# Issuing the selection's transfers from ScalarE instead of SyncE, with a new order of issue

## The chip, the cores and the metric

One core of one Trainium2 chip runs the kernel. The metric is the device time of one execution in microseconds. The kernel before was timed three times: 409.54, 410.28 and 411.35 us, median 410.28 us. One further execution was taken with the hardware profiler.

The engines are called PE (TensorE, the matmuls; PEld are its weight loads), DVE (VectorE), ACT (ScalarE), POOL (GpSimd) and SP (SyncE, which only issues transfers here). Each engine takes its instructions from a queue of its own, strictly in order; "SPq" marks what SP's queue does.

## The reference

Eight sequences of 3136 tokens with 256 channels are filtered in the frequency domain. In each filtered sequence the 128 tokens with the highest scores then go through a small two-layer network.

```python
X = np.fft.rfft(x, axis=1)                       # x: 8 x 3136 x 256
y = np.fft.irfft(X * (filt_r + 1j * filt_i)[None], n=3136, axis=1)
scores = np.einsum('bsd,d->bs', y, w_gate)
out = y.copy()
for b in range(8):
    top = np.argpartition(-scores[b], 128)[:128]  # capacity 128
    xe = y[b, top]
    ye = np.maximum(xe @ w1, 0.0) @ w2            # 256 -> 1024 -> 256
    out[b, top] = xe + sigmoid(scores[b, top])[:, None] * ye
```

## The kernel before, in words

**The filter.** A sequence is cut as 98 x 32 tokens, so that the transform is a product of small matrices. For one batch (one sequence) the work runs as follows. `load` (L506) brings two halves of X, 2 MB together. In eight chunks of 32 channels `outer` (L384) folds X (`add`, `sub`, L401, mostly on POOL), multiplies it (`amm`, L413 to L424, PE) and transposes it into UU (`tout`, L427, DVE). `inner` (L292) takes UU in seven groups: a product (`zmm`, L314, PE), its evacuation to q (`zout`, L318, ACT), two products with the filter (`pmul`, L328, DVE, and `qmul`, L331, POOL), the back transform (`vmm`, L347, PE), its evacuation (`vout`, L361, ACT) and the scores (`gate`, L372, DVE). Then `outer` transposes again (`tin`, L398, DVE), multiplies (`f1`, `f2`, L435, PE, with a two-column copy `fence`, L440, on ACT between them) and evacuates into X (`yout`, L443, ACT), and `store` (L502) writes the half of X out. X exists once: a half is loaded only after its last content was stored. Batch 7 takes a variant of the last step (`fe`, L450, with evacuations `odd`, L458 and L464, on ACT). Three batches are in work at a time: one is loaded and folded, one is filtered, one is transformed back.

**The selection.** `select` (L532) finds the 128 best of a sequence, for batches 0 to 2 together, 3 to 5 together, 6 alone and 7 alone. After the scores are transposed and turned into integer keys in two parts (`s0` to `s5`, DVE and ACT, key tile `kf`), three steps move data:
- `s6` (L583) writes the keys to the buffer `scr` in device memory, in two transfers.
- `s7` (L589) reads `scr` back into the tile `R`, one transfer for each batch of the group and part of the key. Each copies the rows of keys to many partitions. A group of three batches reads its high parts here; batches 6 and 7 read both parts.
- `s8` (L684), for the two groups of three only, reads the low parts into the same `R`, when the high parts are done.

These are 24 transfers: 8 of `s6`, 10 of `s7`, 6 of `s8` (both of the latter in `spread_rows`, L599 to L602). `s7` has to wait until `s6`'s transfers have landed, and until `R` is free. Between them lies a search in rounds: `count` (L627, ACT) counts over `R`, `total` (PE) sums, `over` (L650, L651) and `nextd` set the next threshold. In the middle of the rounds `f8` (L661) and `upper` (L665), both on ACT, finish the high parts, `s8` replaces them in `R`, and `lower` (L669, DVE) adds what `upper` left. The rounds run beside the filter of later batches. Steps `c0` to `c11` then turn the thresholds into row numbers (`idx`).

**The network.** `weights` loads w1 and w2 at the end of the filter, ACT splits them (`whi`, L860) and POOL takes the remainders (`wlo`). `ffn` gathers the selected rows (POOL, indirect transfers, L887), turns them (`turn`, `turned`, L901), multiplies (`up`, L921, and `down`, L946), with `relu` (L931) on ACT, and scatters the result (L954). Batches 0 to 2 begin at about 335 us, while batch 7 is still transformed back.

**The order.** Every step is an entry of the list `prog`, in the order in which `op` is called. `ORDER` (L138) is a hand-fixed list of all 1536 entries: the order in which they are issued, and so the order on each engine's queue. `RINGS` (L212) says for each product which of four PSUM buffers it takes. The entries that matter here: 527, 528, 552 are `s6`, `s7`, `s8` of batches 0 to 2; 989, 990, 1014 those of batches 3 to 5; 1167, 1168 are `s6`, `s7` of batch 6; 1272, 1273 those of batch 7. Of ACT: 1075 and 1068 are the first two `zout` of batch 7, 1012 and 1013 are `f8` and `upper` of batches 3 to 5, 978 and 1120 are `yout` of batches 5 and 6, 620 is a `zout` of batch 4, 1342 is one of the eight `whi`, 1360 the first `relu`. Of SP: 393 loads the second half of batch 4, 517 stores that of batch 2.

Of the kernel before, what the change touches and what calls it, by code (L numbers as in the profile page):

```python
# [47 lines left out]
def _tables(C):  # L48
# [172 lines left out]
def kernel(  # L221
# [310 lines left out]
    def select(bs, st, sts):  # L532
# [50 lines left out]
        def s6():  # L583
            st["scr"] = scr = drm.tile([2, 4, S], F32, name="scr", bufs=2)
            for t in range(2):
                nc.sync.dma_start(out=scr[t, :G].rearrange("g (a c) -> a g c", c=N2),
                                  in_=st[KF][:, t, :GW].rearrange("a (g c) -> a g c", c=N2))
# [523 lines left out]
```

## Time and profile before

| What | us |
|---|---|
| three timed runs | 409.54, 410.28, 411.35 (median 410.28) |
| the profiled execution, its own time | 409.91 |
| its span, first to last instruction | 408.1 |
| PE busy | 384.0 (94%) |
| DVE busy | 348.0 (85%) |
| POOL busy | 306.0 (75%) |
| ACT busy | 239.6 (59%) |
| mean granted clock of TensorE | 0.999 |

The span leaves 409.91 - 408.1 = 1.81 us outside of it. Busy time counts neither waiting nor the issuing of transfers. A matmul's end is modelled, and so 94% does not mean that PE could do no more. Idle time is given in brackets, before the instruction that ended it, with the engine and the line of what it waited for.

### The profile page before, as it was taken

Reading aid. Unit: us, or ns where it says so; the run is one execution under the profiler, and the core shown is the slowest. Engines: PE = TensorE matmul, PEld = TensorE weight load, DVE = VectorE, ACT = ScalarE, POOL = GpSimd, SP = SyncE. Lnnn points to the kernel's source line nnn. Section 1 sums busy time; section 2 is a strip of 40 time slices with the busy share of each in tenths; the row PEclk is TensorE's granted clock in tenths of the full one; section 3 lists DMA queues with packets and bytes.
Section 4 is the critical chain, followed back from the end, with each engine's and each line's share of the span. In section 5 each row is a group of like instructions: output and inputs, shape, how many; then the busy total and the mean of one; then the engine's idle time right before and its main releaser. Section 6 shows DMA issues by size and latency. Waiting matters only on the chain.

```text
span 408.1 us, 11556 instructions
## 1 busy us (share of the span) xinstructions
PE 384.0 (94%) x4666; PEld 215.3 (53%) x4666; DVE 348.0 (85%) x902; ACT 239.6 (59%) x442; POOL 306.0 (75%) x218
## 2 busy tenths in 40 slices
PE   8979799999999999899999999999998989989894
PEld 6445434555544544353454453575344435859794
DVE  2868999989999998879799999999987799888632
ACT  1155235655556578867675554567889985486211
POOL 2367999999897999399959895999179664773262
PEclk9999999999999999999999999999999999999999
DMA  7999950725663654674824565824063556107811
GB/s 287 416 385 411 410 189 32 304 112 208 233 244 145 230 224 180 244 262 188 308 92 207 208 236 230 324 76 207 5 250 118 156 209 246 41 28 214 225 45 34
DMA packets 21957, 83.30 MB, mean 204 GB/s; under 512 B 3472, under 2 KB 13456, under 8 KB 18576
## 3 DMA queue, kind: packets, MB, share of 16 engines
q1 hardware_dynamic: 20912, 80.47, 52.1%
q0 software_dynamic: 992, 2.10, 1.7%
q8 instruction: 37, 0.61, 0.6%
q14 instruction: 16, 0.13, 0.1%
HBM read 47.76 MB, written 34.80 MB: 202 GB/s over the span
## 4 chain that ended last, share of the span: by engine, by line
PE 56%; POOL 10%; DVE 10%; DMA 8%; ACT 7%; issue 7%; SPq 1%; POOLq 0%; ACTq 0%; DVEq 0%
PE ps L435 16%; PE ps L347 13%; PE ps L423 8%; PE ps L314 6%; PE ps L946 4%; PE ps L921 4%; DMA tf_sb<-in_tf_dram 3%; POOL q L331 3%; DMA X<-in_x_dram 2%; POOL X L401 2%; POOL s L401 2%; ACT X L443 2%; DVE rj L372 2%; DMA fb_sb<-in_fri_dram 2%; DVE UU L427 2%
## 5 line engine op out<-in xcount | busy, mean ns | idle before, releaser
L331 POOL TENSOR_TENSOR q<-q,fb_sb 128x1024 f32<-128x1024 f32 (+1 forms) x56 | 119.7, 2142 | 35.4 <-ACT q L318 34.8
L435 PE MATMUL ps<-t,c_sb 64*49 64x512 f32 (+1 forms) x896 | 113.0, 594 | 2.4 <-ACT t L440 1.2
L401 POOL TENSOR_TENSOR s<-X 113x512 f32<-113x512 f32 x57 | 72.5, 1278 | 19.2 <-DMA X<-in_x_dram 15.0
L427 DVE STREAM_TRANSPOSE UU<-ps 128x1024 f32<-128x1024 f32 x64 | 78.3, 1232 | 7.4 <-PE ps L423 7.0
L398 DVE STREAM_TRANSPOSE t<-UU 128x1024 f32<-128x1024 f32 x64 | 78.0, 1226 | 4.7 <-PE ps L435 3.0
L372 DVE SCALAR_TENSOR_TENSOR rj<-ps,wg_sb 128x256 bf16<-128x256 f32 x192 | 69.5, 419 | 9.6 <-PE ps L347 6.6
L443 ACT COPY X<-ps 113x1024 f32<-113x1024 f32 x56 | 56.1, 1012 | 35.0 <-PE ps L435 16.7
L423 PE MATMUL ps<-X,c_sb 49*64 49x512 f32 x324 | 72.4, 595 | 0.5 <-DMA c_sb<-in_cst_dram 0.5
L401 POOL TENSOR_TENSOR X<-X 113x512 f32<-113x512 f32 x53 | 67.5, 1279 | 3.3 <-DVE s L401 0.6
L361 ACT COPY UU<-ps 128x1024 f32<-128x1024 f32 x48 | 48.5, 1012 | 34.4 <-PE ps L347 26.9
L328 DVE TENSOR_TENSOR y<-ps,fa_sb 128x1024 f32<-128x1024 f32 (+1 forms) x56 | 61.2, 1099 | 6.3 <-DMA fa_sb<-in_fri_dram 3.0
L423 PE MATMUL ps<-s,c_sb 49*64 49x512 f32 x244 | 63.1, 596 | 3.5 <-DVE UU L427 2.2
L318 ACT COPY q<-ps 128x1024 f32<-128x1024 f32 (+1 forms) x56 | 51.6, 922 | 21.5 <-PE ps L314 13.0
L347 PE MATMUL ps<-y,ti_sb 64*64 64x256 f32 x768 | 61.2, 380 | 2.8 <-DVE y L328 1.5
L347 PE MATMUL ps<-q,ti_sb 64*64 64x256 f32 x768 | 60.4, 376 | 0.0
L314 PE MATMUL ps<-UU,tf_sb 64*64 64x256 f32 x768 | 52.2, 389 | 2.9 <-DVE UU L427 1.4
L435 PEld LDWEIGHTS ps<-t,c_sb 64*49 64x49 f32 (+1 forms) x896 | 30.5, 125 | 43.2 <-ACT t L440 12.9
L347 PEld LDWEIGHTS ps<-y,ti_sb 64*64 64x64 f32 x768 | 29.3, 132 | 26.1 <-issue 3.9
L314 PEld LDWEIGHTS ps<-UU,tf_sb 64*64 64x64 f32 x768 | 28.4, 132 | 25.0 <-issue 4.6
L347 PEld LDWEIGHTS ps<-q,ti_sb 64*64 64x64 f32 x768 | 30.9, 133 | 11.8 <-POOL q L331 0.9
L423 PEld LDWEIGHTS ps<-s,c_sb 49*64 49x64 f32 x244 | 15.9, 132 | 26.2 <-issue 11.9
L887 POOL DMA_INDIRECT fb_sb<-out_dram,idx x15 | 14.5, 968 | 18.7 <-DVE jk L794 15.3
(132 smaller groups left out, 456.8 us busy)
## 6 DMA issues: line engine op xcount, KB each, us to landing
out_dram<-X SPq DMA_DIRECT2D x16, 2048.0 KB
X<-in_x_dram SPq DMA_DIRECT2D x12, 2048.0 KB
X<-in_x_dram SPq DMA_DIRECT2D x16, 512.0 KB
fb_sb<-in_fri_dram SPq DMA_DIRECT2D x5, 512.0 KB
fa_sb<-in_fri_dram SPq DMA_DIRECT2D x5, 512.0 KB
fb_sb<-in_moe_w_dram SPq DMA_DIRECT2D x2, 1024.0 KB
R<-scr SPq DMA_DIRECT2D x12, 98.0 KB
ti_sb<-in_ti_dram SPq DMA_DIRECT2D x1, 832.0 KB
```

Of the source, the lines that this page charges most:

```text
L314: nc.tensor.matmul(z[o, hi, k * D:k * D + D], lhsT=tf_sb[p, l], rhs=urow(b, l, 0, D)[p], start=True, stop=True)
L318: nc.scalar.copy(out=q[:, :, :n * HW], in_=h["z"][:, :, :n * HW])
L328: nc.vector.tensor_tensor(out=part(y), in0=part(h["z"]), in1=filt(fa_sb), op=ALU.mult)
L331: nc.gpsimd.tensor_tensor(out=part(h["q"]), in0=part(h["q"]), in1=filt(fb_sb), op=ALU.mult)
L347: nc.tensor.matmul(v[o, j, k * D:k * D + D], lhsT=ti_at[p, t, i, hi], rhs=h["yq"[t]][p, hi, k * D:k * D + D], start=t == 0, stop=t == 1)
L372: nc.vector.scalar_tensor_tensor(out=rj, in0=h["v"][:, j, k * D:k * D + D], scalar=1.0, in1=wg_sb, op0=ALU.mult, op1=ALU.mult, accum_out=u ...
L398: nc.vector.transpose(out=h["t"].rearrange("p d (l j) -> p d l j", j=2), in_=uchan(b_out, c))
L401: (nc.gpsimd if fold[k] == "p" else nc.vector).tensor_tensor(out=out, in0=two[0], in1=two[1], op=(ALU.add, ALU.subtract)[k])
L423: nc.tensor.matmul(a[q, w].rearrange("p (n d) -> p n d", d=CW), lhsT=lhs[p], rhs=rhs[p], start=n == 0, stop=n == len(terms) - 1)
L427: nc.vector.transpose(out=uchan(b_in, c), in_=h["a"].rearrange("p w (n d) -> p d n w", d=CW))
L435: nc.tensor.matmul(h["f"][q, s], lhsT=cc["wi"][p, n], rhs=h["t"][p, s * 16:s * 16 + 16].rearrange("p d n -> p (d n)"), start=t == 0, stop= ...
L443: nc.scalar.copy(out=X[:RW2, hx, :, at], in_=h["f"][:RW2].rearrange("p s (d n) -> p n s d", n=N2))
```

## The change

The transfers of `s6`, `s7` and `s8` are issued by `nc.scalar`, that is by ACT's queue, in place of `nc.sync`, SP's queue. What they move is the same. The three steps count as ACT's, so that they stand in ACT's order. `ORDER` and `RINGS` are new: the same 1536 entries, of which most of the others stay where they were or move by a few places on their engine's queue. The diff, with those lines of the old and the new `ORDER` that hold the moved entries (and entry 1075), and without the rest of the list and `RINGS`:

```diff
...
-    451, 522, 398, 397, 406, 452, 523, 524, 484, 409, 453, 407, 525, 399, 410, 526, 408, 527, 412, 416, 400, 411, 467,
...
-    613, 513, 551, 607, 615, 514, 552, 515, 614, 606, 516, 675, 608, 616, 517, 619, 618, 663, 609, 620, 553, 664, 617,
...
-    877, 925, 983, 917, 984, 881, 985, 868, 986, 923, 927, 987, 885, 869, 952, 988, 919, 882, 989, 886, 934, 870, 938,
...
-    1074, 1010, 1164, 1165, 1011, 975, 1166, 1012, 1076, 1167, 1013, 968, 976, 1014, 1075, 977, 1116, 969, 1077, 1067,
...
-    1124, 1035, 1109, 1326, 1125, 1131, 1092, 1110, 1149, 1036, 1111, 1112, 1037, 1132, 1328, 1094, 1327, 1334, 1168,
...
-    1339, 1270, 1360, 1365, 1157, 1052, 1271, 1366, 1053, 1272, 1361, 1226, 1219, 1367, 1054, 1227, 1368, 1055, 1220,
...
-    1175, 1060, 1381, 1176, 1237, 1382, 1177, 1061, 1362, 1273, 1363, 1178, 1063, 1062, 1420, 1238, 1179, 1369, 1370,
...
+    451, 522, 398, 397, 406, 452, 523, 524, 484, 409, 463, 407, 525, 399, 410, 526, 408, 527, 412, 416, 400, 411, 467,
+    417, 401, 464, 453, 468, 393, 528, 469, 418, 419, 413, 470, 466, 430, 415, 454, 420, 431, 471, 456, 414, 455, 432,
...
+    605, 550, 615, 514, 614, 515, 606, 619, 516, 607, 608, 616, 551, 517, 675, 552, 618, 620, 609, 663, 621, 617, 672,
...
+    602, 983, 881, 880, 917, 984, 985, 868, 923, 927, 933, 986, 919, 885, 869, 934, 987, 882, 886, 988, 952, 870, 989,
+    892, 888, 883, 887, 938, 893, 884, 935, 939, 990, 895, 940, 894, 929, 946, 926, 930, 941, 953, 931, 937, 970, 896,
...
+    1010, 1164, 1165, 1074, 1011, 969, 1166, 1116, 975, 1075, 1067, 1012, 1076, 1077, 976, 1013, 977, 1014, 1069,
+    1117, 1126, 1118, 1068, 1119, 978, 1081, 1070, 1121, 1120, 1078, 979, 1015, 1167, 1324, 1016, 1350, 1071, 1083,
...
+    1168, 1150, 1337, 1133, 1093, 1038, 1152, 1134, 1039, 1113, 1151, 1040, 1142, 1351, 1329, 1041, 1135, 1042, 1115,
...
+    1226, 1157, 1360, 1270, 1342, 1052, 1271, 1053, 1365, 1227, 1343, 1361, 1366, 1219, 1054, 1367, 1272, 1055, 1368,
...
+    1180, 1376, 1065, 1181, 1377, 1383, 1239, 1064, 1273, 1386, 1428, 1182, 1183, 1240, 1387, 1066, 1062, 1384, 1184,
...
@@ -583,7 +583,7 @@
         def s6():
             st["scr"] = scr = drm.tile([2, 4, S], F32, name="scr", bufs=2)
             for t in range(2):
-                nc.sync.dma_start(out=scr[t, :G].rearrange("g (a c) -> a g c", c=N2),
+                nc.scalar.dma_start(out=scr[t, :G].rearrange("g (a c) -> a g c", c=N2),
                                   in_=st[KF][:, t, :GW].rearrange("a (g c) -> a g c", c=N2))
 
         def s7():
@@ -599,7 +599,7 @@
         def spread_rows(to, i):
             n = T * K
             for g in range(G):
-                nc.sync.dma_start(out=to[g * n:g * n + n], in_=st["scr"][i, g].rearrange("(k w) -> k w", w=W).partition_broadcast(T))
+                nc.scalar.dma_start(out=to[g * n:g * n + n], in_=st["scr"][i, g].rearrange("(k w) -> k w", w=W).partition_broadcast(T))
 
         def rows_of(ph):
             return st["R"][:np_, ph if alone else 0]
@@ -610,9 +610,9 @@
         for k, f in (("s2", s2), ("s3", s3), ("s4", s4)):
             step("dve", k, f, ["c"], x=[S_])
         step("dve", "s5", s5, w=[KF], x=[S_])
-        step("sp", "s6", s6, [KF], new=("scr", b0))
+        step("act", "s6", s6, [KF], new=("scr", b0))
         held = [("u", 0, l, c) for l in range(4) for c in range(NCH + 1)] if b0 == LAST else []
-        step("sp", "s7", s7, [("scr", b0)], held, new=("R", b0))
+        step("act", "s7", s7, [("scr", b0)], held, new=("R", b0))
 
         R_ = ("R", b0)
         d = cc["dj" if alone else "dj4"]
@@ -681,7 +681,7 @@
             if k == HR - 1:
                 step("act", "upper", upper, [R_, ("fin", b0, 0)], new=("hd", b0))
                 if not alone:
-                    step("sp", "s8", lambda: spread_rows(st["R"][:, 0], 1), [("scr", b0)], [R_])
+                    step("act", "s8", lambda: spread_rows(st["R"][:, 0], 1), [("scr", b0)], [R_])
                 step("dve", "lower", lower, (), [R_], x=[("hd", b0)])
 
         def c0():
```

In the new order ACT's queue runs, around the moved steps (entries left out where nothing hangs on them):

- batches 0 to 2: `zout` 410, **s6** 527, `vout` 400, `zout` 417, `fence` 468, **s7** 528, `yout` 470; later `zout` 613, `f8` 550, `fence` 514, `zout` 606, `yout` 516, `upper` 551, **s8** 552, `zout` 620.
- batches 3 to 5: `zout` 886, **s6** 989, `vout` 883, `zout` 893, `fence` 939, **s7** 990, `fence` 930, `yout` 941; later `yout` 969, `zout` 1075, `f8` 1012, `fence` 976, `upper` 1013, **s8** 1014, `fence` 1118, `zout` 1068, `yout` 978, `yout` 1120, **s6 of batch 6** 1167, `count` 1016.
- batches 6 and 7: `count` 1036, `whi` 1336, **s7 of batch 6** 1168, `fence`, `vout` 1093; then `relu` 1360, `whi` 1342, `odd`, `relu` 1367, **s6 of batch 7** 1272, `odd`; then `count` 1181, 1064 (L799), **s7 of batch 7** 1273, two more of L799, `relu` 1388.

Before, the same part of ACT's queue ran `f8` 1012, `upper` 1013, `fence` 976, `zout` 1075, `yout` 969, `yout` 978, `zout` 1068, `fence` 1118, `yout` 1120, `count` 1016; all eight `whi` stood ahead of `relu` 1360.

## Rows read from the trace of the kernel before

**Rows 1.** The page: busy time and share of each engine.
```profile
PE 384.0 (94%) x4666; PEld 215.3 (53%) x4666; DVE 348.0 (85%) x902; ACT 239.6 (59%) x442; POOL 306.0 (75%) x218
```

**Rows 2.** Busy time by stage: stretch, length, engines, clock, DMA share, GB/s.
```profile
60.00:205.00 145.00, 142.67 (x1930) 70.69 (x1926) 133.50 (x297) 95.12 (x162) 132.25 (x86) 1.00 0.54 212
205.00:290.00 85.00, 83.52 (x1105) 43.14 (x1100) 81.32 (x220) 52.64 (x93) 70.32 (x47) 1.00 0.47 185
295.00:337.00 42.00, 39.10 (x503) 18.05 (x495) 34.90 (x119) 38.04 (x80) 30.32 (x21) 1.00 0.50 178
337.00:387.00 50.00, 46.62 (x329) 37.94 (x329) 41.94 (x162) 27.29 (x70) 24.20 (x23) 1.00 0.51 154
```

**Rows 3.** Transfers by line: count, issue time min/median/max in ns.
```profile
L602 SPq DMA_DIRECT2D R<-scr x14: 585/650/1054, 140.3 to 323.5; - x14
L586 SPq DMA_DIRECT2D scr<-kf x8: 332/406/777, 137.4 to 338.0; - x8
```

**Rows 4.** Timeline of SP's queue: start us, us, what is issued.
```profile
140.29 2.24 SPq L602 DMA_DIRECT2D R<-scr  x3
142.64 0.39 SPq L509 DMA_DIRECT2D X<-in_x_dram  x1
...
170.92 2.46 SPq L602 DMA_DIRECT2D R<-scr  x3
173.89 0.34 SPq L504 DMA_DIRECT2D out_dram<-X  x1
...
294.47 0.76 SPq L586 DMA_DIRECT2D scr<-kf  x2
295.42 2.06 SPq L602 DMA_DIRECT2D R<-scr  x3
...
322.88 1.25 SPq L602 DMA_DIRECT2D R<-scr  x2
...
343.85 1.17 SPq L602 DMA_DIRECT2D UU<-scr  x2
```

**Rows 5.** Waits of SP's queue: us in total, times, longest.
```profile
SPq L504 <- ACT X L443: 120.9, 11, 15.4
...
SPq L602 <- DMA scr<-kf: 7.7, 3, 5.0
```

**Rows 6.** Timeline of ACT: start us, us, instruction, idle before it.
```profile
143.39 1.01 ACT L443 COPY X<-ps 113x1024 f32<-113x1024 f32 x1 [2.38 <-PE ps L423]
...
175.57 1.01 ACT L318 COPY q<-ps 128x1024 f32<-128x1024 f32 x1 [2.24 <-PE ps L314]
...
276.46 1.01 ACT L443 COPY X<-ps 113x1024 f32<-113x1024 f32 x1 [1.28 <-PE ps L423]
...
295.81 1.01 ACT L318 COPY q<-ps 128x1024 f32<-128x1024 f32 x1 [0.20 <-DVE y L328]
...
300.86 1.01 ACT L443 COPY X<-ps 113x1024 f32<-113x1024 f32 x1 [1.21 <-PE ps L435]
...
330.76 0.37 ACT L901 CAST fa_sb<-ps 128x256 fp32r<-128x256 f32 x1 [0.36 <-PE ps L636]
...
333.79 0.66 ACT L860 CAST ti_sb<-fb_sb 128x512 fp32r<-128x512 f32 x1
...
336.13 1.01 ACT L443 COPY X<-ps 113x1024 f32<-113x1024 f32 x1 [1.02 <-PE ps L435]
...
350.26 0.49 ACT L931 ACTIVATE q<-ps 128x384 fp32r<-128x384 f32 x1 [2.25 <-PE ps L946]
...
358.40 0.59 ACT L627 ACTIVATE ps<-UU,c_sb 128x392 f32<-128x392 f32 x1
```

**Rows 7.** POOL: a wait from 60 to 300 us, and its timeline.
```profile
POOL s L401 <- DMA X<-in_x_dram: 3.1, 2, 2.0
...
296.89 2.40 POOL L331 TENSOR_TENSOR q<-q,fb_sb 128x1024 f32<-128x1024 f32 x1 [10.01 <-ACT q L318]
```

**Rows 8.** The page: POOL's gathers, busy us, mean ns, idle before.
```profile
L887 POOL DMA_INDIRECT fb_sb<-out_dram,idx x15 | 14.5, 968 | 18.7 <-DVE jk L794 15.3
```

More of the change, by code (lines that the diff above doesn't have):

```diff
@@ L138 @@
 ORDER = [
[71 rows of a table removed]
[71 rows of a table added]
 ]
 RINGS = (
-    "00120120121203101230120120230123012032031201203120321032302013210321023120312031203103201213012302310231021301"
-    "23023203123101201201321032103210321302130210321321032301023023103120310212031230120102102101203201320132012301"
-    "21030123013201301320321032103203120310210231230103202102123123201202020202031212302320132020312001313113131101"
+    "00120120121203210132013013132301323013012302130123021301021302103210320312031230123210221312013203210321320130"
+    "21321231201322302312031230121030123102130210321321032301032131021301230313021301231213213212310310231203120310"
+    "21030120130213032102301203102201320130230213012312010212023023210212112121320130123123012313021332313113131121"
     "0020"
```

123 rows, old and new, of the table ORDER are left out of this document.

## The prediction

> **What bounds the kernel now.** I read the page first, then busy time by stage, then the queue that the change relieves, then the queue that it loads. Over the whole span PE is busy 94%, DVE 85%, POOL 75%, ACT 59% [rows 1]. An average hides the stages. From 60 to 290 us PE is busy for 226.2 of 230 us, DVE for 214.8, POOL for 202.6 and ACT for 147.8: three engines are near full, ACT is free for more than a third of the time [rows 2]. From 295 to 337 us, where the last batch is filtered while the search of batches 3 to 5 runs its second half, this turns round: ACT is busy 38.04 of 42.00 us, 3.96 us idle, and DVE and POOL have more room [rows 2]. From 337 to 387 us ACT is busy 27.29 of 50 us. So time on ACT is cheap everywhere but in this one stage.
>
> SP's own queue is no bound. Its longest waits are for work on other engines: its stores wait 120.9 us in total for the evacuations that fill X [rows 5]. The search's transfers do hold up other transfers a little. The load of batch 4's second half starts at 142.64 us, right behind the three issues of `s7` that began at 140.29 us and took 2.24 us, and the store of batch 2's second half at 173.89 us stands behind the three issues of `s8`, 170.92 us plus 2.46 us [rows 4]. But who waits for a load? POOL folds X, and its waits for X from 60 to 300 us come to 3.1 us in two places [rows 7].
>
> **What the change moves, and its price on ACT.** The steps go to ACT with every issue: 8 x 0.406 us for `s6`, 14 x 0.650 us for the reads into R, and 1.17 us for the last two [rows 3, 4]. That is 3.25 + 9.10 + 1.17 = 13.5 us by SP's medians. No row shows an issue on ACT. From below it costs nothing, where the queue issues while the instruction before still computes. From above I take the nearest row of an engine that computes and issues, POOL's indirect gathers with 0.968 us each [rows 8]: 24 x 0.968 = 23.2 us. I take SP's durations, because the shapes and the form of the transfer are the same as there, and keep both ends for the range.
>
> What of it lies beside idle time of ACT, slot by slot in the new order:
> - Batches 0 to 2, `s6` and `s7`: `s7` stands right ahead of the `yout` that found 2.38 us of idle time before it, against 2.24 us of issuing [rows 4, 6]. `s6` follows an evacuation of 1 us during which PE is the one that is waited for. Cost nothing. If PE came earlier, the cost would be the 2.24 us.
> - The same batches, `s8`: it stands ahead of the `zout` that had 2.24 us of idle time, against 2.46 us [rows 4, 6]. Cost 0.2 us at most; POOL has other work queued ahead of the product that needs this `zout`. Cost nothing.
> - Batches 3 to 5, `s6` and `s7`: as long as the pair at 294.47 and 295.42 us, 0.76 + 2.06 us [rows 4]; `s6` follows an evacuation again, and the idle time before the next `yout` is 1.28 us [rows 6]. The `fence` behind `s7` would come 0.8 us late, but in the new order PE has other products to do before it needs it. Cost nothing, 0.8 us if PE gets there earlier.
> - Batches 3 to 5, `s8` (2.06 us), batch 6, `s6` (0.76 us) and `s7` (1.25 us) [rows 4]: these fall into the full stage. Together 4.07 us, beside 3.96 us of idle time in the whole stage. Of that idle time only what lies behind the slots helps: 1.21 us ahead of the `yout` at 300.86 us, and 0.36 and 1.02 us at 330.76 and 336.13 us, 2.59 us [rows 6]. 4.07 - 2.59 = 1.48 us stay uncovered. One `whi` (the 0.66 us at 333.79 us, less 0.04 us that such instructions overlap [rows 6]) is moved behind the first `relu`, out of the stage: 1.48 - 0.62 = 0.86 us.
> - Batch 7, `s6` and `s7` (two issues of at most 0.777 us [rows 3], and 1.17 us): behind 337 us, ACT idles for nearly half of the stage, and the gap ahead of the `relu` at 350.26 us alone is 2.25 us [rows 2, 6]. `R` of batch 7 comes some 4 us later than before, but its first `count` ran only at 358.40 us [rows 6], some 13 us after the old issue at 343.85 us [rows 4]. Cost nothing.
>
> Waits are moved too. `s7` waits until `s6` has landed, and on ACT evacuations stand behind this wait. SP waited 7.7 us in three places for that, 5.0 us in the longest [rows 5]. The longest is that of batch 7, where `s6` was issued right behind a store. The other two sum to 2.7 us, and in the new order two evacuations stand between `s6` and `s7` of each group of three, some 2 us. I take the price as nothing and 2.7 us as its upper end, both ends lying in stages where ACT has room.
>
> **What leaves SP.** 13.5 us of issuing and the waits above. The load at 142.64 us can start earlier by at least the issue of `s7` (2.24 us) and at most by 2.24 + 2.7 us; the store at 173.89 us by at most the 2.46 us. POOL was not waiting there. Gain nothing.
>
> Here a rule speaks on the change. The Trainium skill, "DMA: Bandwidth & Descriptors", section "Issuing engines are not separate DMA queues", says that transfers of all issuing engines share the same 16 DMA engines, and that a second issuing engine saves only the sequencer's time of issue. By the rule the load gains 2.24 us; by the rows it can gain up to 4.9 us, because the queue also stood still for a landing. Either way nobody waits for it, and the sum is the same.
>
> **The order.** The other entries move by few places. One move is plain to price: the first `zout` of batch 7 stood behind `f8` and `upper`, and started at 295.81 us; POOL had waited 10.01 us for it [rows 6, 7]. Now it stands ahead of both. `f8` and `upper` together take 1.2 us, so it may come up to 1.2 us earlier. But the second `zout` of that batch now stands behind `s8`, 0.9 us or so later, and PE works on both in order. I count the two as even.
>
> **The sum.** 409.91 us (the profiled execution: span 408.1 and 1.81 us around it) + 0.86 us = 410.77 us. The median of the three timed runs is 0.37 us above the profiled one, and I forecast against the median: 410.28 + 0.86 = 411.1, said as 411.0 us. A measurement of this kernel can tell about 0.5% from no change, 2.05 us: below 408.2 us is faster, above 412.3 us slower.
>
> **Rivals.**
> 1. *The new order and earlier transfers pay.* POOL's 3.1 us of waits for X go [rows 7], or the 1.2 us at batch 7's beginning are kept and the second `zout` is not late, with like gains at the other ends of batches. For it: three engines near full, so each gap that closes in all three is a gain. Against it: the loads that come earlier are not those that POOL waited for. Price about 3 us: 410.28 - 3.0 = 407.3 us.
> 2. *ACT becomes the bound from 295 to 337 us (slower).* The 4.07 us of issuing find no cover, because the idle time there belongs to waits that move along with the delay: if the `yout` at 300.86 us and the `zout` behind it are only as late as their inputs, and those are made by PE from what ACT evacuates, each delay comes round again. It decides from the point at which the added issuing exceeds the stage's idle time, and 4.07 against 3.96 us is on the edge. 410.28 + 4.07 = 414.4 us.
> 3. *The change doesn't do what it says:* SP's queue is not freed in effect, because the waits for landings are now ACT's, and each holds evacuations. 2.7 us of waits plus half the issuing of the full stage gone uncovered, say 410.28 + 2.7 + 0.5 = 413.5 us. An issue on ACT of 0.968 us would end in the same place: seven in the full stage make 6.8 us, less the 2.59 and 0.62 us, 413.9 us.
>
> **How the numbers follow.** Forecast 0.44, rival 1 0.28, rival 2 0.20, rival 3 0.08. The forecast's own range is 409.0 to 412.8 us; it gives 0.02 to faster, 0.36 to same, 0.06 to slower. Rival 1, centred on 407.3 us, gives 0.25 to faster and 0.03 to same. Rivals 2 and 3 give 0.03 to same and the rest, 0.25, to slower. So faster 0.27, same 0.42, slower 0.31. For 8 times in 10 the range takes in both main rivals and the upper price of an issue: 406.0 to 415.0 us.
>
> **What would show it.** Right: the issues appear on ACT, 0.4 to 0.7 us each; POOL's waits for X stay near 3 us; in the stage that was 295 to 337 us ACT's idle time shrinks to 2 us or less, and the stage is about 1 us longer; stages before 290 us are within 0.5 us. Wrong: an issue on ACT near 1 us; waits of ACT for `scr` above 1 us each; the first `up` of batches 0 to 2 more than 2 us later (rival 2), or stages between 60 and 290 us shorter by more than 1 us (rival 1). A change of more than 1 us in the first 60 us would come from the new order of the first loads, which I hold for even, since all of them have to land in any case.

## The result and the profile after

The changed kernel takes 416.5 us (median of 416.12, 416.15, 416.84 and 417.71), the kernel before 410.81 us beside it: a ratio of 1.0147, 95% interval 1.0110 to 1.0183. It is slower by about 6 us, where I forecast 411.0 us and a range of 406.0 to 415.0 us. The profiled execution has a span of 415.1 us against 408.1, and a mean granted clock of TensorE of 0.989 against 0.999.

The page of the changed kernel, its busy time and the queue that is new (packets, MB, share of 16 engines):

```profile
PE 387.1 (93%) x4666; PEld 215.0 (52%) x4666; DVE 348.4 (84%) x902; ACT 240.1 (58%) x442; POOL 306.4 (74%) x218
...
q10 hardware_dynamic: 2736, 2.21, 1.9%
```

Against [rows 1] the engines do the same work; PE's 3.1 us more go with the lower granted clock. The same stages as [rows 2], moved by the delay:

```profile
64.00:212.00 148.00, 143.74 (x1926) 70.34 (x1918) 133.47 (x296) 95.36 (x161) 131.12 (x86) 0.99 0.53 204
212.00:297.00 85.00, 83.67 (x1118) 42.07 (x1118) 82.23 (x222) 53.58 (x95) 70.25 (x47) 1.00 0.49 189
302.00:344.00 42.00, 37.09 (x489) 17.52 (x482) 33.86 (x114) 35.76 (x80) 29.32 (x20) 1.00 0.49 178
344.00:394.00 50.00, 46.68 (x333) 38.44 (x331) 42.12 (x165) 28.61 (x71) 25.31 (x24) 1.00 0.51 154
```

The first stage is 3 us longer for the same work, the second equal, the third has PE and ACT some 2 us less busy in 42 us, the last is equal.

Where the time went is read best by taking the two traces entry by entry. For each entry of `ORDER`, the time of its first instruction in one trace less that in the trace before; of these the median over all that began, before, in 10 us. I call this the **shift**. A step in it is a place where time is lost; where it is level, both kernels run alike. For the changed kernel and the runs of the next section (us):

```
before's us  after  h1    h2    h3    h4    j2    j3    j4     k1    n1    p1    p2    n3
   20         4.2   0.5   2.3   0.3   1.4   1.6   1.3   1.4    1.6   4.0   2.1   1.3   0.4
  100         4.0   1.1   2.1   0.0   0.9   1.4   1.2   1.5    1.2   3.6   1.7   1.9  -0.8
  160         4.2   1.3   2.0   0.0   1.3   1.6   1.2   1.7    1.4   3.8   1.9   1.8  -0.8
  200         7.3   4.4   7.0   1.3   6.1   5.6   2.0  11.3    4.4   4.3   5.0   3.3   0.3
  290         6.3   3.4   6.2   1.3   5.1   4.6   1.1  10.4    3.5   3.3   4.0   2.4  -0.5
  340         7.7   4.9   6.6   4.7   6.9   6.0   1.4  11.8     -    3.7   5.5   3.0  -0.1
  400         6.9   4.1   5.8   4.7   5.9   5.2  -0.7   9.6     -    1.7   4.5   2.2  -2.2
```

In the changed kernel there are three steps: 4.0 us in the first 25 us, 3.1 us between 160 and 200, 1.4 us between 290 and 340; 1.0 us goes back between 200 and 290 and 0.8 us behind 340. 4.2 (at 160 us) + 3.1 - 1.0 + 1.4 - 0.8 = 6.9 us, against 7.0 us between the spans.

**The first step: the head.** Windows of 2 us of the changed kernel (columns as in [rows 2]: stretch, length, PE, PEld, DVE, ACT, POOL, granted clock, DMA share, GB/s):

```profile
14.00:16.00 2.00, 0.48 (x8) 0.00 (x0) 2.00 (x3) 0.00 (x0) 1.27 (x1) 1.00 1.01 412
16.00:18.00 2.00, 1.76 (x12) 0.83 (x16) 0.74 (x1) 0.00 (x0) 0.00 (x0) 0.61 0.95 358
18.00:20.00 2.00, 2.00 (x15) 0.81 (x12) 0.13 (x1) 0.00 (x0) 0.00 (x0) 0.53 0.74 259
```

PE is busy 0.48 of 2 us, then the granted clock is 0.61 and 0.53, near the lower of TensorE's two levels (1.2 of 2.4 GHz). In the new order the third chunk of batch 0, whose load is issued last, is multiplied sixth instead of fourth. PE's matmuls stand for 1.8 us (its weight loads for 2.6 us), and the first weight load of that product begins at 16.21 us, 0.09 us after SP's queue saw the load of the chunk land (16.12 us; the same 0.09 us in h2 and h4). The matmuls that follow take 1.06 us each at the lower clock, in place of 0.59.

```profile
PE ps L423 <- DMA X<-in_x_dram: 1.8, 1, 1.8
```

**The second step.** The waits of DVE and PE from 168 to 192 us (total, times, longest), and ACT's timeline there:

```profile
DVE y L328 <- ACT q L318: 3.3, 2, 2.7
DVE R L669 <- DMA R<-scr: 2.0, 1, 2.0
...
PE ps L314 <- ACT UU L361: 3.0, 1, 3.0
```

```profile
175.96 1.02 ACT L443 COPY X<-ps 113x1024 f32<-113x1024 f32 x1
177.01 0.92 ACT L665 ACTIVATE ps<-R,fin 96x784 f32<-96x784 f32 x1
177.96 3.56 ACTq L602 DMA_DIRECT2D R<-scr  x3
181.61 1.01 ACT L318 COPY q<-ps 128x1024 f32<-128x1024 f32 x1 [3.69 <-POOL s L401]
182.52 1.02 ACT L361 COPY UU<-ps 128x1024 f32<-128x1024 f32 x1
```

ACT issues `s8` of batches 0 to 2 for 3.56 us, and the `zout` 620 of [rows 6] stands behind it. Its 2.24 us of idle time before are gone: `upper` is no longer ahead of `zout` 606 and `yout` 516 but behind them. The 3.69 us in brackets are the issues, whatever releaser is named. DVE then waits twice: for this read-out, and in `lower` for the rows that `s8` brings. PE stands for 3.0 us, and behind that its granted clock is low again for a while:

```profile
184.00:186.00 2.00, 2.00 (x20) 1.01 (x16) 0.14 (x1) 0.83 (x2) 2.00 (x2) 0.50 0.85 237
186.00:188.00 2.00, 2.00 (x19) 0.60 (x15) 2.00 (x8) 0.84 (x2) 1.52 (x2) 0.72 0.75 279
```

The clock is not what makes this step: in h1 and k1 PE stands for the same 3.0 us, the granted clock stays at 1.00 there, and the step is as long (3.1 and 3.0 us).

**The issues themselves** (ns: min/median/max) cost on ACT what they cost on SP [rows 3], save two that take 1.4 us, both in this `s8`, and one of 1.2 us at 347 us:

```profile
L602 ACTq DMA_DIRECT2D R<-scr x14: 602/665/1427, 144.8 to 330.9; - x14
L586 ACTq DMA_DIRECT2D scr<-kf x8: 320/431/1223, 141.5 to 347.4; - x8
```

### The profile page after: what moved, and what is told of

Its sections match the earlier page's. It is cut to its first block, busy times and chain, and to the rows that moved or that the text cites. A ratio compares the mean times of both kernels' runs of the same rounds, so it can differ in the third digit from the quotient of the medians.

```text
span 415.1 us, 11553 instructions
## 1 busy us (share of the span) xinstructions
PE 387.1 (93%) x4666; PEld 215.0 (52%) x4666; DVE 348.4 (84%) x902; ACT 240.1 (58%) x442; POOL 306.4 (74%) x218
## 4 chain that ended last, share of the span: by engine, by line
PE 63%; DVE 11%; ACT 7%; issue 6%; DMA 5%; POOL 3%; ACTq 2%; SPq 1%; POOLq 0%; DVEq 0%
PE ps L435 18%; PE ps L347 15%; PE ps L423 11%; PE ps L314 8%; PE ps L921 4%; PE ps L946 4%; DMA fb_sb<-in_fri_dram 3%; DVE t L398 3%; DVE UU L427 2%; ACT X L443 2%; DVE rj L372 2%; DMA X<-in_x_dram 2%; POOL out_dram L954 2%; ACTq L602 2%; ACT q L318 2%
## 5 line engine op out<-in xcount | busy, mean ns | idle before, releaser
L435 PE MATMUL ps<-t,c_sb 64*64 64x512 f32 (+1 forms) x896 | 115.7, 598 | 4.1 <-ACT t L440 1.9
L423 PE MATMUL ps<-X,c_sb 49*64 49x512 f32 x324 | 73.8, 618 | 1.8 <-DMA X<-in_x_dram 1.8
L318 ACT COPY q<-ps 128x1024 f32<-128x1024 f32 (+1 forms) x56 | 51.5, 922 | 26.7 <-PE ps L314 14.5
L361 ACT COPY UU<-ps 128x1024 f32<-128x1024 f32 x48 | 48.2, 1014 | 23.5 <-PE ps L347 19.1
L314 PE MATMUL ps<-UU,tf_sb 64*64 64x256 f32 x768 | 53.2, 393 | 5.9 <-ACT UU L361 3.0
L435 PEld LDWEIGHTS ps<-t,c_sb 64*64 64x64 f32 (+1 forms) x896 | 31.1, 126 | 44.9 <-issue 13.9
L347 PEld LDWEIGHTS ps<-q,ti_sb 64*64 64x64 f32 x768 | 29.8, 133 | 13.1 <-POOL q L331 1.9
```

Of the source, the lines that this page charges most:

```text
L314: nc.tensor.matmul(z[o, hi, k * D:k * D + D], lhsT=tf_sb[p, l], rhs=urow(b, l, 0, D)[p], start=True, stop=True)
L318: nc.scalar.copy(out=q[:, :, :n * HW], in_=h["z"][:, :, :n * HW])
L347: nc.tensor.matmul(v[o, j, k * D:k * D + D], lhsT=ti_at[p, t, i, hi], rhs=h["yq"[t]][p, hi, k * D:k * D + D], start=t == 0, stop=t == 1)
L423: nc.tensor.matmul(a[q, w].rearrange("p (n d) -> p n d", d=CW), lhsT=lhs[p], rhs=rhs[p], start=n == 0, stop=n == len(terms) - 1)
L435: nc.tensor.matmul(h["f"][q, s], lhsT=cc["wi"][p, n], rhs=h["t"][p, s * 16:s * 16 + 16].rearrange("p d n -> p (d n)"), start=t == 0, stop= ...
```

## The experiments

The runs are named by a letter and a number. In the kernels of the runs a line stands 5 to 9 lines lower than in the changed kernel (L669 is L678, L602 is L611, L318 is L324). A diff shows the entries moved or the choice of issuer; `ON_ACT` holds the steps that ACT issues, by the first batch of their group. Ratios are to the kernel before, run beside it, with 95% intervals. `RINGS` always goes with the order: 188 of the 334 products of the changed kernel follow another product in their PSUM buffer than before, and where a run mixes the two orders, all but a few products at the seam follow the one that they follow in the order they are taken from. No run separates the buffers from the order.

```diff
+        def issuer(s):
+            return nc.scalar if (b0, s) in ON_ACT else nc.sync
...
-                nc.scalar.dma_start(out=to[g * n:g * n + n], ...
+                issuer("s7" if i == 0 or alone else "s8").dma_start(out=to[g * n:g * n + n], ...
```

### Which part of the change makes the loss

**h1: the first 64 entries in the old order.** Diff: `ORDER = old[:64] + new[64:]`, all on ACT.

> The changed kernel with the first 64 of its 1536 entries in the order of the kernel before (entries and set are the same 64: the loads of batch 0, its fold, the tables); all transfers stay on ACT. Theory (two places): between the two traces the same instructions stand 4.0 us later from 20 us on, which is the order of the first entries; undone here, so 416.5 - 4.0 = 412.5 us, and the second shift, at 175 us, stays. Rival A (ACT's issues make all of it): no place in the first 64 entries issues on ACT, so 416.5. Rival B (the shift of the head is hidden again by a later wait): 415 to 416.5.

Measured 414.99 us (413.96 to 419.28), ratio 1.0143 (1.0074 to 1.0212). The shift is 0.5 us at 20 us and 1.1 at 100, not 0 and not 4; the other two steps stay (3.1 and 1.5). So most of the head's 4.0 us went, but the timed runs gained only 1.5 us, within their scatter.

**h2: the new order, SP issues.** Diff: `ON_ACT = set()`.

> The new order whole, with all 24 transfers issued by SP again, each at its place in the new order. Theory: the 4.0 us of the head stay, the 3.6 us in which ACT issued the second rows of batches 0 to 2 at 178 us are gone, and so are the 3.3 us of issues in the stage that ACT fills (worth about 1): 416.5 - 3.5 = 413 us, 412 to 414. Rival A (the issues on ACT make all of it): 410.8. Rival B (the new order makes all of it, whoever issues): 416.5.

Measured 415.02 us (414.74 to 415.64), ratio 1.0107 (1.0065 to 1.0149). My theory failed: without any issue on ACT the second step grew, from 3.1 to 5.0 us. The waits from 168 to 192 us of DVE and of PE:

```profile
DVE R L678 <- DMA R<-scr: 5.0, 1, 5.0
...
PE ps L429 <- DVE R L678: 4.1, 1, 4.1
```

`lower` (553) stands on DVE for the rows, and PE's next product (665) takes the PSUM buffer that `lower` frees. Behind this stop the granted clock is 0.51 from 186 to 188 us and 0.63 from 188 to 190. SP's timeline:

```profile
168.29 0.34 SPq L515 DMA_DIRECT2D X<-in_x_dram  x1
174.84 0.34 SPq L510 DMA_DIRECT2D out_dram<-X  x1
175.75 3.55 SPq L611 DMA_DIRECT2D R<-scr  x3
```

The rows are asked for 4.8 us later than before (170.92 us, [rows 4]), of which 2.0 us is the head, and behind the 2 MB store instead of ahead of it.

**h3: the old order, ACT issues.** Diff: `ORDER = old`, `ON_ACT` = all.

> The old order whole, with the 24 transfers issued by ACT, each at its old place. Theory: nothing of the head; the second rows of batches 0 to 2 stand ahead of a read-out of ACT that waited 2.24 us in the old trace, so 0 to 1.4 us of their 2.5 to 3.6; in the stage that ACT fills, 0.9 to 1.5: 411.7 to 413.5 us. Rival A (the issues make all of it): 416.5. Rival B (the new order makes all of it): 410.8.

Measured 415.9 us (414.63 to 417.05), ratio 1.0140 (1.0093 to 1.0187): by itself the issuing engine costs as much as the whole change. The shift is 0.0 up to 160 us, so the issues at 140 us are covered. It steps by 1.3 us at 170 and by 3.4 between 290 and 340, more than twice the 0.9 to 1.5 that I expected. ACT's timeline there:

```profile
295.79 0.77 ACTq L594 DMA_DIRECT2D scr<-kf  x2
296.61 0.91 ACT L673 ACTIVATE ps<-R,fin 96x784 f32<-96x784 f32 x1 [0.72 <-DMA scr<-kf]
297.46 0.18 ACT L445 COPY t<-t 128x2 f32<-128x2 f32 x1
297.55 2.06 ACTq L610 DMA_DIRECT2D R<-scr  x3
299.65 1.01 ACT L323 COPY q<-ps 128x1024 f32<-128x1024 f32 x1 [2.01 <-DVE t L403]
```

0.77 + 2.06 us of issues stand ahead of the first `zout` of batch 7, which is behind them and late by nearly all of it.

**h4: one step back on SP.** Diff: `ON_ACT` without `(0, "s8")`.

> The changed kernel with one step, the second rows of batches 0 to 2 (three transfers at 178 us), issued by SP again at the same place in the order. Theory: ACT is not held for 3.6 us ahead of the read-out for batch 4, TensorE does not stand for 3.0 us behind it: 416.5 - 3.5 = 413.0 us. Rival A (the issues cost evenly, 13.5 us over 24): a gain of at most 0.6, 415.9. Rival B (the read-out's buffer, not the issue, held it): 416.5.

Measured 416.11 us (415.65 to 417.69), ratio 1.0147 (1.0100 to 1.0194). The theory fell here too: the step at 175 us is 4.8 us, close to h2's 5.0, and DVE waits 4.8 us for the rows. ACT's hold was taken away and the wait of `lower` was next.

```profile
DVE R L678 <- DMA R<-scr: 4.8, 1, 4.8
```

### The place at 175 us

**j2: `upper` and `s8` as early as before.** `551, 552` moved directly behind 550:

```diff
-... 550, 615, 514, 614, 515, 606, 619, 516, 607, 608, 616, 551, 517, 675, 552, 618, 620 ...
+... 550, 551, 552, 615, 514, 614, 515, 606, 619, 516, 607, 608, 616, 517, 675, 618, 620 ...
```

> The changed kernel with two entries moved: the multiply by the upper part and the second rows of batches 0 to 2 (551, 552) go directly behind 550, as early as in the old order, ahead of two read-outs of ACT; all on ACT. Theory: the rows land some 5 us earlier, the subtraction on VectorE (553) does not wait, and the read-out for batch 4 finds ACT free; the shift at 175 to 190 us is 1.3 as with the old order and ACT's issues instead of 3.2: 416.5 - 1.9 = 414.6 us. Rival A (ACT is held for 3.5 us wherever it issues them): 416.5. Rival B (the transfer's landing is late for the loads and stores beside it, not for its place): the wait of VectorE stays at 2 us, 416.

Measured 416.21 us (415.07 to 418.39), ratio 1.0151 (1.0098 to 1.0204). `lower` no longer waits, and the step is still 4.0 us: rival A. The waits of DVE and of PE, 168 to 192 us:

```profile
DVE y L334 <- ACT q L324: 3.5, 1, 3.5
...
PE ps L441 <- ACT t L446: 3.2, 1, 3.2
```

ACT is held for 2.57 us ahead of another `zout` and a `fence`, for which PE waits.

**j3: SP issues, `lower` later.** Diff: 553 moved behind 667, `ON_ACT = set()`. Product 665 then takes another PSUM buffer, which does not wait for `lower`; the run shows the two together.

> The new order with all transfers on SP (415.0 measured) and one entry moved: VectorE's subtraction of the second rows (553) goes six of VectorE's and TensorE's entries later, behind the read-out 667. Theory: in the new order with SP that subtraction waited 5.0 us for its rows, and TensorE 4.1 us for the tile that it frees; moved, neither waits, and the shift at 180 us falls from 4.8 to under 1: 410.3 to 411.5 us. Rival A (the rows are needed as much by what comes next, the count 554): 414 to 415. Rival B (the shift has to do with the new order of the matrix work there, not with the rows): 415.

Measured 409.73 us (408.74 to 410.93, ten runs), ratio 0.9964 (0.9933 to 0.9994): the theory, with 0.6 us more gained than it allowed. One entry (with its buffer) turns the new order from 1.1% slower to 0.4% faster. Not all of it is this place: from h2 to j3 the shift at the end falls by 6.5 us, of which 4.2 us is the step at 175 us, 0.9 us the head, whose code is the same, and 1.4 us a gather of POOL that landed sooner in this trace (last section). DVE's wait for the rows:

```profile
DVE R L678 <- DMA R<-scr: 0.2, 1, 0.2
```

The step is 0.8 us; kernels whose entries there are old and on SP show 0.1 to 1.1 (n4, k4, n3), so no more is left than those have.

**j4: `s8` behind `zout` 627, `lower` behind 657, on ACT.**

> The changed kernel with two entries moved later: the second rows of batches 0 to 2 (552) behind the third read-out for batch 4 (627), and VectorE's subtraction (553) behind the fold's read-out 657. Theory: ACT's 3.6 us of issuing no longer stand ahead of the read-out 620, whose delay left TensorE idle for 3.0 us; the shift at 175 to 190 us falls from 3.2 to about 1: 414.3 us. Rival (the rows then land too late for the count 554 and the selection's chain, and ACT stands on it): 416 to 419.

Measured 419.38 us (414.75 to 420.5), ratio 1.0181 (1.0102 to 1.0260): the rival, slightly above its range. ACT is no longer held by the issues, but the rows come too late for `lower` and for the search's next `count`, and DVE, PE and ACT stand:

```profile
DVE R L678 <- DMA R<-scr: 5.9, 1, 5.9
...
PE ps L353 <- DVE R L678: 7.0, 1, 7.0
...
ACT ps L636 <- DVE R L678: 7.2, 1, 7.2
```

**k1: `lower` later, all on ACT** (j3 with ACT).

> The changed kernel, all 24 transfers on ACT, with VectorE's subtraction of the second rows of batches 0 to 2 (553) behind the read-out 667; the same move took the new order on SP from 415.0 to 409.7 us. Theory (two prices in one place: the rows land late for 553, and ACT's 3.6 us of issues stand ahead of the read-out 620): the wait of VectorE goes, TensorE's 3.0 us behind the read-out stay, so the shift at 175 to 190 us stays at 2.5 to 3.5: 415 to 416.5 us. Rival (the late rows alone were the price, ACT's issues are covered): the shift falls to 1, 411 us.

On this chip, where k1 to k4 ran, TensorE's granted clock was 0.97 to 0.99 in nearly all executions and the kernel before took 416.38 to 427.48 us, so that the undisturbed part of the traces (up to 290 us) counts and the ratios say little. k1: 431.18 us against 423.77 us, ratio 1.0137 (1.0082 to 1.0193). The step at 175 us is 3.0 us, as the theory has it: DVE no longer waits for the rows, PE waits for ACT as in the changed kernel.

```profile
PE ps L320 <- ACT UU L367: 3.0, 1, 3.0
...
DVE y L334 <- ACT q L324: 3.3, 2, 2.7
```

**k2: as k1, but `s8` of batches 0 to 2 on SP.**

> As the new order on SP with 553 moved (409.7 us), but 21 of the 24 transfers on ACT: all save the second rows of batches 0 to 2. Theory: the issues up to 160 us and at 278 to 283 us cost nothing; those in the stage that ACT fills (second rows of batches 3 to 5, both steps of batch 6) cost 0.9 to 1.5, as between the changed kernel and the new order on SP: 410.6 to 411.2 us, shift 0 against the SP form up to 295 us. Rival (each issue on ACT costs): 409.7 + 21 x 0.56 = 421, or half of that, 415.

430.32 us, ratio 1.0139 (1.0074 to 1.0205) on the same chip, no better than k1's: the time that I expected was not measured. The step at 175 us is gone (0.5 us), and up to 290 us the shift is level with j3's, as the theory has it. Behind 290 us the run can't show more: up to 340 us k2 loses 4.1 us, but k4, with all transfers on SP, loses 2.7 us there too, at a granted clock of 1.00, where n3, with the same order in that stretch, loses 0.4 us on another chip.

**p1 and p2: the store behind the rows.** 517 (the 2 MB store) moved behind 552, once with ACT issuing and once with SP:

```diff
-... 616, 551, 517, 675, 552, 618 ...
+... 616, 551, 675, 552, 517, 618 ...
```

> The changed kernel with one entry moved: the store of batch 2's second half (517, 2 MB, SP's queue) behind the second rows of batches 0 to 2 (552, on ACT) instead of ahead of them, as in the old order. In six traces with the store issued 0.9 us ahead the three issues took 3.55 to 3.65 us, in four without it 2.05 to 2.57. Theory (the new order of store and rows lengthens the issue and the landing): the issue falls to 2.0 to 2.6 us, VectorE's wait for the rows from 2.0 to under 0.5, and the shift at 175 to 190 us from 3.1 to 2.0: 415.4 us. Rival (the store does not matter): issue 3.6, shift 3.1, 416.5.

> The new order on SP (415.0) with the same one entry moved: the store 517 behind the second rows 552, both on SP's queue. Theory: the rows no longer stand behind 2 MB; they land some 3 to 5 us earlier, VectorE's wait of 5.0 us falls under 1.5, the shift at 175 to 190 us from 5.0 to 1.5 or less: 411 to 412 us. Rival (the rows are late because the multiply ahead of them, 551, came 4 us later): the wait stays above 3 us, 414 to 415.

With SP 411.21 us (410.66 to 413.82, ten runs), ratio 1.0023 (1.0004 to 1.0042): the theory. SP's timeline, and what is left of DVE's wait:

```profile
175.60 2.14 SPq L611 DMA_DIRECT2D R<-scr  x3
177.78 0.44 SPq L510 DMA_DIRECT2D out_dram<-X  x1
```

```profile
DVE R L678 <- DMA R<-scr: 1.2, 1, 1.2
```

With ACT 414.8 us (414.38 to 417.77), ratio 1.0124 (1.0077 to 1.0172), and the place is unchanged: the step 3.1 us, the issue 3.55 us, the wait 1.9 us. The edit could not work, and I should have seen it: on two queues the list no longer orders the two, SP issued the store at 174.78 us as soon as it could, and ACT the rows at 175.70.

### Covered issues, the head, and the other half

**n1: 14 of 24 on ACT.** As j3, with `s6` and `s7` of batches 0 to 2, 3 to 5 and 7 on ACT. These are 14 transfers (5, 5 and 4), not the 12 of the expectation; its rival's 6.7 us are then 7.8 us.

> The new order with VectorE's subtraction (553) moved and SP issuing (409.7 us there), but 12 of the 24 transfers on ACT: both first steps of batches 0 to 2, of 3 to 5 and of batch 7. Left on SP are the second rows of both groups and all of batch 6, the places where ACT was short. Theory (an issue on ACT costs where ACT is short, not as such): the shift against the SP form stays under 0.3 us throughout, 409.7 to 410.2 us. Rival (each issue costs, 0.56 us): 12 x 0.56 = 6.7, 416.4; or half of that, 413.

Measured 410.14 us (408.79 to 411.88, ten runs), ratio 0.9988 (0.9961 to 1.0014). From 160 to 290 us its shift falls by 0.5 us, that of j3 by 0.1, and behind 290 us both run alike: those issues cost nothing. The theory holds, though this trace has the whole 4.0 us in its head, where nothing is issued by ACT.

**j1, k3, n2: more of the head old.** j1: `old[:240] + new[240:]` on ACT (the 240 entries end at 84 us, not at 55 to 60 as the expectation says). k3: the same with j3's move, on SP. n2: `old[:545]` and j3's move, on SP.

> The changed kernel with its first 240 entries in the old order (the first 55 to 60 us), all else and the transfers on ACT as changed. The same new head stood at 4.0, 2.1 and 1.0 us behind the old one in three profiled executions, and with 64 old entries it still stood at 1.1. Theory: with 240 old entries the shift is 0 up to 170 us, and the later shifts (3.2 at 175 us, 1.4 at 300, -0.8 behind) stay: 410.8 + 3.8 = 414.6 us, below the 416.5 of the changed kernel. Rival (the new head costs nothing, what differed was the clock granted in each execution): 416 to 416.5.

> The new order on SP with 553 moved (409.7 us) and the first 240 entries (84 us) in the old order. Theory: the new head costs 1.0 to 1.3 us at an undisturbed clock: 408.5 us, 0.5 to 0.7% below the kernel before. Rival (the head's new order costs nothing): 409.7.

> All transfers on SP, 553 moved, the first 545 entries (166 us) in the old order, the rest new. Theory: the new head costs 1.2 us at an undisturbed clock, so 409.7 - 1.2 = 408.5 us, and the ratio to the kernel before 0.992 to 0.995. Rival (the head's cost is given back by 170 us anyway): 409.7.

j1: 415.59 us (413.2 to 417.7), ratio 1.0120 (1.0054 to 1.0187). k3, on the chip of k1: 426.21 us, ratio 0.9969 (0.9921 to 1.0017), weak like the others there. n2: 410.5 us (407.49 to 412.9), ratio 0.9999 (0.9974 to 1.0025). In the traces the old head stands between -0.8 and 0.7 us, the new one between 0.7 and 4.2; in the timed medians the difference does not stand out, and n2 is not below j3. These runs don't settle the head's price.

**n4: the first 64 entries new, the rest old, on SP.**

> The kernel before with its first 64 entries (to 23 us) in the new order, all transfers on SP. Theory: the new head alone costs 1.0 us where TensorE's clock stays, 2 to 4 where it falls in the idle stretch at 13 to 16 us or behind: 411.8 to 414 us, more scattered than the kernel before. Rival (the head's shift came from entries behind the first 64): 410.8.

Measured 416.7 us (414.97 to 418.35), ratio 1.0158 (1.0126 to 1.0190), and it does not measure what it should. Its shift is 1.3 us at 20 us and 5.1 from 40 us on, from a wait that only this pairing has: DVE's next entry of the old order reads a load that the new order issues 8.7 us later (23.01 instead of 14.31 us).

```profile
DVE cr_sb L1007 <- DMA UU<-in_cst_dram: 6.2, 1, 6.2
```

**k4, n3: where the new order gains.** SP issues, `old[:699] + new[699:]` and `old[:774] + new[774:]`.

> All transfers on SP, the first 699 entries (210 us) in the old order, the rest in the new one. Theory: what the new order gains lies behind 270 us (in the new order on SP with 553 moved the shift against the kernel before fell from 2.0 at 210 us to -0.7 at the end): 410.8 - 2.5 = 408.3 us. Rival (that gain needs the new order of the first half): 410.8.

> All transfers on SP, the first 774 entries (231 us) in the old order, the rest new. Theory: what the new order gains lies behind 231 us, 1.0 to 2.5 us (with 553 moved the shift fell from 1.9 at 230 us to -0.7 at the end, with 699 old entries from 0.4 to -0.5 at 290): 408.3 to 409.8 us. Rival (the gain needs the new order of the earlier part): 410.8.

k4 ran on the chip of k1: 424.46 against 423.77 us, ratio 1.0131 (1.0048 to 1.0214); with that chip's loss behind 290 us it says nothing of the gain. n3: 407.88 us (406.35 to 410.48, twelve runs), ratio 0.9938 (0.9911 to 0.9965). The kernel with nothing of the change but the order behind 231 us is 0.6% faster than the kernel before, and the best version that I ran.

## Why the prediction was wrong, point by point

**The price of an issue on ACT** was right. 665 and 431 ns at the median are SP's 650 and 406; three of the 24 issues exceeded the upper bound of 0.968 us.

**"Cost nothing" for `s6` and `s7`** of both groups and of batch 7 was right: the shift is level at 140 us in h3, and level with j3's in n1. The waits for landings that moved to ACT cost nothing either.

**"Cost nothing" for `s8` of batches 0 to 2** is the step that failed most, in two ways. I took the cover, 2.24 us of idle time ahead of `zout` 620, from the trace before, and did not ask whether the new order leaves it there. It does not: `upper` now comes behind `yout` 516, so that ACT has work up to the moment at which it begins to issue. And I took 2.46 us for the issue; it was 3.56. The hold costs 3.0 us with no wait for the rows beside it (k1), against 0.5 us with `s8` on SP (k2). Nor is an earlier place free: 1.3 us at the old place in the old order (h3), 4.0 directly behind `f8` in the new one (j2).

**A term was missing: who waits for the rows of `s8`.** I priced the waits ahead of the transfers and never the landing behind them. `lower` on DVE reads what `s8` brings and frees the buffer of PE's next product. The new order asks for the rows some 3 us later (beside the head's delay) and lets the store go first, but keeps `lower` nearly in its place. The new `RINGS` has a part in it: before, the next product in the buffer that `lower` frees was 668, now it is 665. This costs 5.0 us with SP (h2), 1.5 with the store behind (p2), no more than the old entries with `lower` moved (j3). With ACT it does not add to the hold, since both are the same microseconds: 3.1 us with it (after, h1), 3.0 without (k1). That is why h4, which took away one of the two, gained nothing.

**Two engines, one set of DMA engines.** The rule that I cited, the Trainium skill's "DMA: Bandwidth & Descriptors", section "Issuing engines are not separate DMA queues", that transfers of all issuing engines run on the same 16 DMA engines, agrees with the landing here: `lower` found the rows 7.9 us after their first issue with ACT issuing (177.96 to 185.86 us) and 8.1 us with SP (175.75 to 183.88), each time behind the store, and 4.3 us after it in p2, where the store came later (175.60 to 179.91). A second queue did not bring the rows past the store.

**The full stage** was right in kind and somewhat small: 0.86 us forecast, 1.4 measured (1.4 to 1.8 in h1, h4, j2, j4 and p1), of which 0.3 to 0.6 us is there with SP too (h2, j3, n1, p2), so about 1.0 us for the issues. In the old order it would have been rival 2: 3.4 of its 4.07 us. (Rival 3's sum is off on its own terms: half of 4.07 us is 2.0, not 0.5.)

**The head, "even, since all of them have to land in any case",** failed. That they all land says nothing of when the last one lands that the next product needs. The same code cost 0.9 us at 100 us in h4, whose granted clock stays at 1.00 in the head, 2.1 in h2, where it is 0.55 and 0.59 from 22 to 26 us, and 4.0 in the changed kernel. Of the 3.1 us between h4 and the changed kernel, 1.1 us is the landing of that load (14.99 against 16.12 us); the lower clock behind it goes with the rest. What the head adds to the timed median stays open.

**The rest of the order** was not even: n3, with the new order behind 231 us alone, gains 2.5 us (timed, 0.62% of 411 us; its shift falls by 2.5 us too, from 0.3 to -2.2). The changed kernel has that order as well, but its shift falls by 0.8 us behind 340 us, n3's by 2.1. The difference is the gather of the last section, which landed 1.4 us sooner in n3's trace and not by the order, since the changed kernel, h1 and h2 have the same order there. About 1 us of n3's gain is then the order's, as far as the traces show; whether the timed runs had the short gather is not known.

**A sign that failed.** POOL's waits for X, which were to stay near 3 us, came to 6.6 us from 64 to 308 us in the changed kernel. They are not the price: j3, faster than the kernel before, has 7.1 us from 60 to 310.

As a table of issue against order, by the timed ratios: old order on ACT 1.0140, new order on SP 1.0107, both 1.0147; new order with `lower` moved on SP 0.9964, on ACT 1.0137. So ACT's issuing costs 1.4% in the old order. In the new one with `lower` moved it costs 3.0 us at 175 us by k1's trace, while k1's ratio, from its chip, is weak. Most of the order's 1.1% is the rows of one step (4.2 of the 6.5 us between h2 and j3). The two prices don't add, because they fall into the same place. None of my rivals had either at 175 us.

## What to carry to other kernels

Idle time that is to hide a moved step must be read in the new order's queue, entry by entry, not in the old trace: the reordering that comes with a move may have filled it. Price a transfer at both ends, what stands behind its issue on the queue and who reads what it brings, with what else is in flight just ahead of it. When undoing one suspected part gains nothing, look for the wait that took its place before calling the part innocent.

## What the runs showed of the hardware that I had not expected

**An issue takes longer behind a large transfer, on another engine's queue too.** The three issues of `s8` took 3.54 to 3.66 us in the twelve traces in which SP had issued the 2 MB store 0.9 us earlier, with ACT issuing (after, h1, j1, k1, p1) and with SP (h2, h4, j3, k2, k3, n1, n2); where the store came later, or 5 us earlier, they took 2.05 to 2.57 us (before, h3, j2, j4, k4, n3, n4, p2). With SP one swap shows it: 3.55 us in h2, 2.14 in p2. With ACT it is by comparison of kernels alone. The changed kernel's store:

```profile
177.04 0.34 SPq L504 DMA_DIRECT2D out_dram<-X  x1
```

**The same code, another clock.** After PE's stop in the head the granted clock was 0.53 to 0.61 in the changed kernel and 1.00 in h4, whose head is the same code:

```profile
14.00:16.00 2.00, 1.37 (x17) 0.46 (x13) 2.00 (x3) 0.00 (x0) 1.27 (x1) 1.00 1.02 415
16.00:18.00 2.00, 2.00 (x24) 0.99 (x20) 1.64 (x2) 0.00 (x0) 0.00 (x0) 1.00 0.88 279
18.00:20.00 2.00, 2.00 (x19) 0.79 (x12) 1.54 (x2) 0.93 (x1) 0.00 (x0) 1.00 0.82 290
```

The stop was not equally long: in h4 PE was busy 1.37 us of the 2 us from 14 to 16, in the changed kernel 0.48. At 180 us it was: PE stood for 3.0 us in the changed kernel, p1, h1 and k1, and the granted clock behind it fell to 0.50 in the first two (184 to 186 and 182 to 184 us) and stayed at 1.00 in the other two. It also fell behind longer stops at that place, in j2 (0.50 from 176 to 178 us), j4 (0.50 from 188 to 196), h2 (0.51 from 186 to 188) and h4 (0.50 from 186 to 188). What decides it the runs don't show.

**A gather's landing has two lengths.** The last part of POOL's gather for batch 6 landed 5.9 to 6.3 us after its second issue ended in eleven traces (before, after, h1 to h4, j1, j2, n4, p1, p2) and 4.6 to 4.7 us in five (j3, j4, n1, n2, n3), and these five are 1.4 us earlier from 385 us on; those of k1 to k4 are left out. What decides it the runs don't show.
